# The phases of the states as one product in place of three, with every tile at a fixed place in two large tiles

## The chip, the cores and the metric

The kernel runs on one core of a Trainium2 chip. The metric is device time in microseconds of one execution. The kernel before took 527.39 us (median of three runs, 527.39 to 527.72).

The core has a matrix engine (PE; its weight loads are listed apart as PEld), a vector engine (DVE), a scalar engine (ACT), a general engine (POOL) and a queue engine (SP) that only issues DMAs. Each engine works through its own list of instructions in order. Where one needs another's result, it waits on a semaphore: the built program gives each waiting instruction a semaphore and the count that it must reach.

## The reference

One input `u` of 2048 rows by 640 channels goes through two branches, and a gate mixes them. Branch A is a convolution whose kernel K is a sum over 128 complex states per channel; branch B filters a two-dimensional Fourier transform.

```python
    def _A_ref(u, log_A_real, A_imag, C_real, C_imag, log_dt, D_skip):
        dt = jnp.exp(log_dt)
        A = -jnp.exp(log_A_real) + 1j * A_imag
        C = (C_real + 1j * C_imag) * dt[:, None]
        P = jnp.exp((A * dt[:, None])[:, :, None] * pos[None, None, :])
        K = 2.0 * jnp.einsum("dn,dnl->dl", C, P).real
        ...
        y = jnp.fft.irfft(Uf * Kf[None, :, :], L2)[:, :, :L]
        return y + u * D_skip[None, None, :]
    def _B_ref(x, w_r, w_i):
        X = jnp.fft.rfft2(x, axes=(-2, -1)) * (w_r + 1j * w_i)
        return jnp.fft.irfft2(X, s=(S, D), axes=(-2, -1))
    ...
    return g * a + (1 - g) * b
```

For each state the kernel needs the sine and cosine of an angle for all 2048 positions. It splits the position in an inner and an outer part, and forms each angle in turns. The whole turns have to be taken off before the sine: adding a large constant and taking it off again rounds the number of turns x to a whole one, and what is wanted is that whole number minus x.

## The kernel before, in words

There are four stages. **Phase A** (`phase_a`) transforms `u` over the positions and stores it to DRAM as `u_d`. **Phase P** (`phase_p`) prepares the parameters of the states and stores them, cut in three bfloat16 parts each, to the DRAM tensors `par_d0` (angles) and `par_d1` (decays). **Phase B** (`phase_b`) makes K from them, interleaved with **the channel branch** (`channels`, `filt`, `back1`, `back2`), which is the rest of branch B. **Phase D** (`phase_d`) transforms K (L370, then L383), multiplies it with the spectrum of `u` (L869, L870, L875), transforms back (L900, copied by ACT at L902), stores the half result to the DRAM tensor `s3_d` (L909), loads it in another layout as the tile `t3` (L948, in `load_c`) and finishes with the products at L973 and the gate.

Phase B runs over 40 tiles t, 16 channels each. Two products on the rows of `par1` and an exponential (`mags`, L709 and L710) give the decays `e`. Then `phases` makes the angles twice, for the outer part (`sc`, L725) and the inner part (L731). In `phases` (L713 to L720) three matrix products pile up in the same PSUM bank: with the first table come x and the rounding constant, with the second the constant's negative, with the third minus x. Each of the three is two products on 64 rows and 512 columns (partitions 0 to 63 and 64 to 127), so there are six at L719 for each call, and 80 calls. `prods` (L739 to L745) multiplies decays and angles on DVE and POOL, and `kgen` (L758) sums over the states. `load` brings `par1` (L696, two DMAs) and `par0` (L698, one DMA) for five tiles at a time, issued by POOL.

The tile `t3` spreads over the partitions in steps of four: each of its loads writes every fourth partition, 32 in all.

```python
                T.ld = eng.dma_start(t3s[c][y::4, :, a:a + w], src[:, :, a:a + w])
```

There are 16 such loads from SP and one from ACT. Of these, 15 move 640 KB and two (the halves of the last) 320 KB.

The order on every engine is written out by hand: `arrange` reads one list of numbers per engine (`ORDER`) and ties each engine's instructions in that order, and `CROSS` adds some ties between engines where two tiles share a place. Tiles come from pools of the framework, each a tensor of its own. The framework finds which accesses of a tensor overlap and sets the waits from that.

Of the kernel before, what the change touches and what calls it, by code (L numbers as in the profile page):

```python
# [9 lines left out]
F32 = mybir.dt.float32  # L10
BF = mybir.dt.bfloat16
# [3 lines left out]
PSUM = bass.MemoryType.PSUM  # L15
# [35 lines left out]
def _tables():  # L51
# [72 lines left out]
    one_row[:, :, 0] = 1.0  # L124
    rm = np.zeros((2, 64, 8, 96))
    rp = np.zeros((2, 32, 8, 128))
    for x in range(8):
        g, i = x // 4, 6 * (x % 4)
        rp[g, i:i + 3, x, 0:32] = rp[g, i:i + 3, x, 32:64] = j + 0.5
        rp[g, i:i + 3, x, 64:96] = rp[g, i:i + 3, x, 96:128] = 64 * j  # L130
        rp[g, i + 3:i + 6, x, 64:128] = 1.0
        rp[g, 24, x, 32:64] = rp[g, 24, x, 96:128] = -0.25
# [3 lines left out]
    rq = rp.copy()  # L136
    for x in range(8):
        rq[1 - x // 4, 24, x] = MAGIC
    flat = lambda v: np.concatenate([v[..., 0:64].reshape(64, 512), v[..., 64:128].reshape(64, 512)], 1)
    rn = np.zeros((64, 512))  # L140
    rn[24] = -MAGIC
    rp = np.tile(np.concatenate([flat(rq), rn, flat(-rp)], 1), (2, 1))
# [25 lines left out]
class Ctx:  # L168
    pass

# [28 lines left out]
def body(tc, A, out):  # L199
    nc = tc.nc  # L200
    T = Ctx()
    with ExitStack() as top:
        dram = top.enter_context(tc.tile_pool(name="dram", bufs=1, space=DRAM))
        T.u_d = dram.tile([4, 128, 17, 2, 160], F32, name="u_d")
# [22 lines left out]
        with ExitStack() as cctx:  # L227
            def left():
                with ExitStack() as ctx:
                    T.bc = ctx.enter_context(tc.tile_pool(name="b_c", reuse_waits="tile", bufs=1))  # L230
                    T.rm = T.bc.tile([128, 768], BF, name="rm")
                    T.rp = T.bc.tile([128, 2560], BF, name="rp")
                    yield from phase_p(tc, A, T)
                    yield from phase_b(tc, A, T, ctx)
# [13 lines left out]
            arrange(tc)  # L248
# [422 lines left out]
def phase_b(tc, A, T, ctx):  # L671
# [12 lines left out]
    par_v = [t.rearrange("y x i z n -> y (x i) z n") for t in T.par_d]  # L684
    steps = rp[:, 0:1024], rp[:, 1024:1536], rp[:, 1536:2560]
# [5 lines left out]
    def load(b0):  # L691
        for k in (1, 0):
            par = w2.tile([128, BT, N], BF, tag="par%d" % k, name="par%d" % k)
            if k:
                for j in range(2):
                    G.dma_start(par[64 * j:64 * j + 48], par_v[1][b0 // BT, 48 * j:48 * j + 48])  # L696
            else:
                G.dma_start(par[:, :, :], par_v[0][b0 // BT])  # L698
            for t in range(b0, b0 + BT):
                pars[k][t] = par[:, t - b0, :]  # L700
# [12 lines left out]
    def phases(t, c, n):  # L713
        p = ps.tile([128, 2, 512], F32, tag="ps", name="p_p")
        for i, w in enumerate(steps):
            y = 0 if i == 1 else c
            for j in range(2):
                x = slice(64 * j, 64 * j + 64)
                P.matmul(p[:, j, 0:n], pars[0][t][x], w[x, y:y + n], start=i == 0, stop=i == 2)  # L719
        return p  # L720

    def outer(t, r):
        p = phases(t, 512, 512)
# [4 lines left out]
    def inner(t, r):  # L728
        p = phases(t, 0, 512)
# [309 lines left out]
def arrange(tc):  # L1039

    nc, traced_by = tc.nc, {}
    for name, text in ORDER.items():
        traced = [i for i in nc.cur_bb.bb.instructions if i.engine == getattr(mybir.EngineType, name) and "Boundary" not in type(i).__name__]
        seq = []
        for part in text.split():
            a, _, n = part.partition("+")
            seq += traced[int(a):int(a) + int(n or 1)]
        assert len(seq) == len(traced) == len({i.name for i in seq})
        for a, b in zip(seq, seq[1:]):
            tc.add_manual_dep(b, a.name, NOSYNC, reason="order")  # L1050
        traced_by[name] = traced
    for pair in CROSS.split():
        (e, i), (f, j) = ((x[0], int(x[1:])) for x in pair.split(">"))
        tc.add_manual_dep(traced_by[LETTER[f]][j], traced_by[LETTER[e]][i].name, NOSYNC, reason="slot")


ORDER = {
    "PE": """
# [20 lines left out]
""",  # L1079
    "DVE": """  # L1080
# [74 lines left out]
```

## Time and profile before

| what | value |
|---|---|
| median of three runs | 527.39 us |
| profiled execution, first to last instruction | 526.1 us |
| granted PE clock, mean of the core | 0.992 |
| PE busy in the span | 492.4 us (94%) |
| DVE busy | 432.3 us (82%) |
| ACT busy | 308.1 us (59%) |
| POOL busy | 275.8 us (52%) |
| moved by DMA | 100.55 MB, mean 191 GB/s |

Times come from one profiled execution. Busy time is the union of an engine's instructions, idle time before an instruction is put down to what ended it, and the granted clock is the share of full speed that PE was given.

### The profile page before, as it was taken

How to read it: one execution, taken by the hardware profiler on the slowest of the kernel's cores; microseconds unless marked ns; L12 is line 12 of the kernel's file. 1: busy time of each engine (PE TensorE's matmuls, PEld its weight loads, DVE VectorE, ACT ScalarE, POOL GpSimd, SP SyncE). 2: the span in 40 equal slices, each digit the busy share in tenths (PEclk: the TensorE clock that was granted, in tenths of full speed). 3: DMA queues.
4: the chain of work that ended last, by engine and by line, in shares of the span. 5: the costliest groups of instructions: out<-in, count | busy, mean ns of one | idle time of the engine just before them, and what ended most of it. 6: DMA issues, size and time to landing. Idle time of an engine off the chain costs nothing. (4 is left out here: it accounts for less than half of the span.)

```text
span 526.1 us, 17188 instructions
## 1 busy us (share of the span) xinstructions
PE 492.4 (94%) x7448; PEld 365.2 (69%) x7448; DVE 432.3 (82%) x678; ACT 308.1 (59%) x484; POOL 275.8 (52%) x294
## 2 busy tenths in 40 slices
PE   8869999997889989999999899999999999999896
PEld 6859877765656656656656566757979879988641
DVE  0699757879999998999979869964797977979954
ACT  3566265577886787885976886877323333332210
POOL 4087626428637346476256345156452667538750
PEclk9989999999999999999989999999999999999999
DMA  8926753375251232541312421139689899889974
GB/s 337 403 103 212 284 184 116 106 241 186 78 198 52 75 109 67 190 141 52 98 61 62 165 60 29 56 121 411 215 293 349 276 328 329 296 265 355 310 257 173
DMA packets 47827, 100.55 MB, mean 191 GB/s; under 512 B 3620, under 2 KB 33080, under 8 KB 46088
## 3 DMA queue, kind: packets, MB, share of 16 engines
q1 hardware_dynamic: 25176, 67.41, 36.4%
q10 hardware_dynamic: 20080, 22.52, 13.0%
q0 software_dynamic: 2496, 9.54, 5.0%
q8 instruction: 58, 0.95, 0.7%
q14 instruction: 17, 0.14, 0.1%
HBM read 60.12 MB, written 39.65 MB: 190 GB/s over the span
## 5 line engine op out<-in xcount | busy, mean ns | idle before, releaser
L383 PE MATMUL p_s<-t,w 128*64 128x160 f32 x1056 | 89.0, 307 | 3.6 <-ACT ut L418 3.4
L383 PEld LDWEIGHTS p_s<-t,w 128*64 128x64 f32 x1056 | 75.6, 135 | 12.8 <-ACT ut L418 4.3
L744 POOL TENSOR_TENSOR y<-e,sc 128x512 f32<-128x512 f32 x40 | 53.4, 1335 | 34.5 <-ACT sc L725 34.4
L719 PE MATMUL p_p<-rp,par 64*128 64x512 bf16 x480 | 63.3, 382 | 5.7 <-ACT sc L725 2.6
L710 ACT ACTIVATE e<-p_e 128x1024 f32<-128x1024 f32 (+1 forms) x80 | 61.7, 823 | 9.4 <-issue 4.5
L745 POOL TENSOR_TENSOR y<-e,sc 128x512 f32<-128x512 f32 x40 | 53.5, 1338 | 21.7 <-ACT sc L725 21.6
L371 ACT COPY t<-p_s 128x512 f32<-128x512 f32 x40 | 25.1, 627 | 48.2 <-PE p_s L370 42.7
L731 ACT ACTIVATE p_p<-p_p 128x1024 f32<-128x1024 f32 x40 | 40.5, 1013 | 15.8 <-PE p_p L719 12.4
L741 DVE TENSOR_TENSOR x<-e,p_p 128x1024 f32<-128x1024 f32 x40 | 48.4, 1211 | 0.0
L902 ACT COPY s<-p_i 128x640 f32<-128x640 f32 x32 | 22.1, 692 | 39.6 <-PE p_i L900 33.4
L758 PEld LDWEIGHTS p_k<-x,y 128*32 128x32 f32 x2560 | 37.6, 110 | 10.5 <-issue 8.2
L758 PE MATMUL p_k<-x,y 128*32 128x64 f32 x2560 | 44.1, 220 | 0.1
L739 DVE SCALAR_TENSOR_TENSOR x<-e,p_p 128x512 f32<-128x512 f32 x40 | 27.2, 680 | 20.5 <-ACT p_p L731 20.5
L725 ACT ACTIVATE sc<-p_p 128x1024 f32<-128x1024 f32 x40 | 41.0, 1026 | 4.6 <-PE p_p L719 4.4
L719 PEld LDWEIGHTS <-par 64*128 64x128 bf16 x480 | 20.7, 95 | 32.2 <-issue 13.6
L900 PE MATMUL p_i<-t,w 128*64 128x160 f32 x528 | 42.2, 300 | 0.9 <-DVE t L875 0.7
L370 PE MATMUL p_s<-c,kt 128*64 128x128 f32 x640 | 42.6, 273 | 0.2 <-PE p_s L383 0.2
L875 POOL TENSOR_TENSOR t<-ma 64x320 f32<-64x320 f32 x32 | 28.4, 887 | 26.5 <-DVE ma L869 25.3
L370 PE MATMUL p_s<-c,u 128*64 128x128 f32 x640 | 39.4, 277 | 2.5 <-ACT t L418 2.3
L370 PEld LDWEIGHTS p_s<-c,kt 128*64 128x64 f32 x640 | 38.0, 136 | 4.3 <-issue 3.0
L900 PEld LDWEIGHTS p_i<-t,w 128*64 128x64 f32 x528 | 36.4, 136 | 6.5 <-issue 2.6
L370 PEld LDWEIGHTS p_s<-c,u 128*64 128x64 f32 x640 | 36.0, 138 | 6.6 <-issue 3.2
(165 smaller groups left out, 1017.2 us busy)
## 6 DMA issues: line engine op xcount, KB each, us to landing
u_d<-ut SPq DMA_DIRECT2D x32, 320.0 KB, 3.6
us<-u_d ACTq DMA_DIRECT2D x16, 640.0 KB, 5.5
s_d<-s ACTq DMA_DIRECT2D x15, 640.0 KB, 7.8
t<-s_d SPq DMA_DIRECT2D x14, 640.0 KB, 5.5
ww<-in_w_l SPq DMA_DIRECT2D x8, 642.0 KB, 4.3
ue<-u_d SPq DMA_DIRECT2D x8, 640.0 KB, 5.5
k_d<-kt SPq DMA_DIRECT2D x4, 1280.0 KB, 5.9
kt<-k_d SPq DMA_DIRECT2D x8, 640.0 KB, 6.0
```

Of the source, the lines that this page charges most:

```text
L370: nc.tensor.matmul(p[64 * ri:64 * ri + 64, j, :], src(i + j), e1[ri], start=True, stop=True)
L383: ins = nc.tensor.matmul(p[64 * j:64 * j + 64, i, 160 * ri:160 * ri + 160], w2[:, x, 64 * ri:64 * ri + 64], t1[:, x // 2 if x < 32 else K0 ...
L710: st.exp = S.activation(ef[:, :, c:c + n], p[:, :, 0:n], AF.Exp)
L719: P.matmul(p[:, j, 0:n], pars[0][t][x], w[x, y:y + n], start=i == 0, stop=i == 2)
L725: S.activation(sc.rearrange("p d v i -> p (d v i)"), p.rearrange("p j w -> p (j w)"), AF.Sin, scale=TWO_PI)
L731: T.trig = st.trig = S.activation(f, f, AF.Sin, scale=TWO_PI)
L741: V.tensor_tensor(out=x[:, 0].rearrange("p d (h j) -> p d h j", h=2), in0=e[:, :, 0:64].rearrange("p d (h j) -> p d h j", h=2), in1=cx.uns ...
L744: G.tensor_tensor(out=y[:, 1], in0=e[:, :, 64:96], in1=sc[:, 0], op=ALU.mult)
L745: G.tensor_tensor(out=y[:, 0], in0=e[:, :, 64:96], in1=sc[:, 1], op=ALU.mult)
L758: P.matmul(st.pb[32 * r:32 * r + 32, o, :], y[:, ri, 4 * qq + JR[r], :], x[:, ri, 4 * qq + JR[r], :], start=t % 2 + qq + 1 - ri == 0, stop ...
L875: return eng.tensor_tensor(out=t2[64 * im:64 * im + 64, o, :], in0=m[l, :hn, 0, :], in1=m[l, :hn, 1, :], op=ALU.add if im else ALU.subtract)
L900: T.mm = P.matmul(p[x:x + 64, i // 2, 160 * (i % 2):160 * (i % 2) + 160], T.w3[:, k0 + h + i, x:x + 64], t2[:, h + i, :], start=True, stop ...
```

## The change

Two things change. First, the products of `phases`: each angle row now stands in the table as x in rows 0 to 23, the quarter turn in row 24, the constant in row 25, its negative in row 26 and minus x in rows 32 to 63, so that one product per half does what three did. The eight tables become four, the columns of a product 256 instead of 512, and the parameters come in two groups g side by side in the free dimension. The tile `rp` shrinks from 2560 to 512 columns, `par0` doubles, and its load becomes four DMAs.

```diff
-    one_row[:, :, 0] = 1.0
+    one_row[:, :, 0:3] = 1.0
...
+    rp[32:64] = -rp[0:32]
+    rp[25], rp[26] = MAGIC, -MAGIC
...
-                G.dma_start(par[:, :, :], par_v[0][b0 // BT])
+                    for x in (0, 32):
+                        G.dma_start(par[64 * j + x:64 * j + x + 32], T.par_d[0][b0 // BT, 2 * j:2 * j + 2].rearrange("g i z n -> i g z n"))
...
-        for i, w in enumerate(steps):
-            y = 0 if i == 1 else c
+        for g in range(2):
             for j in range(2):
                 x = slice(64 * j, 64 * j + 64)
-                P.matmul(p[:, j, 0:n], pars[0][t][x], w[x, y:y + n], start=i == 0, stop=i == 2)
+                P.matmul(p[:, j, n * g:n * g + n], pars[0][t][x, g], rp[x, c:c + n], start=True, stop=True)
```

Second, how the program is written down. `body` no longer calls the framework: a class `Program` records every operation, `lay` gives each pool a stretch of addresses, and `write` then issues the operations in one list of numbers for all engines, putting each tile at a place in two tiles that fill the whole memories, `sbuf` and `psum`. `arrange` and the ties of `CROSS` are gone.

```diff
+        for s, n in self.SIZE.items():
+            pool = self.area.enter_context(self.tc.tile_pool(name=s, bufs=1, **({"space": PSUM} if s == "psum" else {})))
+            area[s] = pool.tile([128, n // 4], F32, name=s)
...
+                x = area[s][:, h.slot[1] // 4:h.slot[1] // 4 + size]
...
+        for n in order:
+            op = self.ops[n]
...
-            arrange(tc)
+        tc.write(sequence(ORDER))
```

Line by line, the instructions of DVE, ACT and SP stand in the same order as before. On PE only the products of `phases` differ, on POOL only the loads of the parameters. What differs besides is what instructions wait for. Three places follow; the words in brackets are the semaphores that an instruction waits for, one for each engine and some (DMAHW, DMASW) for DMAs.

On POOL, near the start of phase B, these are the first loads of the parameters before (par_521 and par_1015 are `par1`, par_524 and par_1018 are `par0`).

```order
L430 TENSOR_TENSOR z<-c_66,gw 128x640 [waits PE_49,Pool_49]
L696 DMA par_1015<-par_d_62 48x640 [waits DMASW1_49]
L696 DMA par_1015<-par_d_62 48x640 [waits DMASW2_49]
L698 DMA par_524<-par_d_61 128x640 [waits DMASW6_49,DMASW5_49]
L698 DMA par_1018<-par_d_61 128x640
```

The same place of the changed kernel, where every tile on the chip is called sbuf or psum:

```order
L865 DMA sbuf<-par_d_62 48x640 [waits DMASW1_49]
L865 DMA sbuf<-par_d_62 48x640 [waits DMASW2_49]
L868 DMA sbuf<-par_d_61 32x2x640 [waits DMASW6_49,DMASW5_49]
L868 DMA sbuf<-par_d_61 32x2x640 x3
L868 DMA sbuf<-par_d_61 32x2x640 [waits DMASW7_49]
L868 DMA sbuf<-par_d_61 32x2x640 [waits DMASW0_49]
```

Each load at L698 is now four at L868, and the later ones of the eight wait for the loads just ahead.

On SP in phase D, these are the first loads of `t3` before (L948; t_6040 is `t3`, s_d is `s3_d`), between those of K (L816) and of another tile (L936).

```order
L936 DMA t3e<-s3e_d 128x2560 [waits DMAHW4_49,DMAHW1_49,PE_49]
L948 DMA t_6040<-s_d 32x5120 [waits DMAHW3_49,DMAHW0_49,DVE_49]
L816 DMA kt<-k_d 128x1280 [waits DMAHW7_49,PE_49,Pool_49]
L948 DMA t_6040<-s_d 32x5120 [waits DMAHW4_49]
L948 DMA t_6040<-s_d 32x5120 [waits DMAHW3_49,DMAHW2_49]
```

The same place of the changed kernel, in which L1117 is L948, L985 is L816 and L1105 is L936:

```order
L1105 DMA sbuf<-s3e_d 128x2560 [waits DMAHW4_49,DMAHW1_49,PE_49]
L1117 DMA sbuf<-s_d 32x5120 [waits DMAHW2_49,DMAHW1_49,DMAHW3_49,DMAHW0_49,DMAHW5_49,DVE_49,DMAHW6_49,PE_49,DMAHW7_49,Activation_49,Pool_49]
L985 DMA sbuf<-k_d 128x1280 [waits DMAHW3_49,PE_49]
L1117 DMA sbuf<-s_d 32x5120 [waits DMAHW5_49,DMAHW4_49,DMAHW6_49,DVE_49,DMAHW7_49,Activation_49,Pool_49]
L1117 DMA sbuf<-s_d 32x5120 [waits DVE_49,DMAHW1_49,PE_49,DMAHW2_49,Activation_49,Pool_49]
```

The loads stand where they stood. The first now waits for all eight semaphores of SP's and ACT's DMAs but one, and for all four engines; the counts in the built program are those of the instruction that stands just ahead of the load in the list, on each engine.

On PE, at the same place, these are the products of the back transform before (L900; p_i_5877 and p_i_5891 are two PSUM banks, t_5659 the spectrum).

```order
L900 MATMUL p_i_5877<-t_5659,w_5003 64x160 [waits DMAHW5_49]
L900 MATMUL p_i_5877<-t_5659,w_5003 64x160
L900 MATMUL p_i_5891<-t_5659,w_5003 64x160 [waits Activation_49,Pool_49]
L900 MATMUL p_i_5891<-t_5659,w_5003 64x160 x7
L383 MATMUL p_s_5907<-t_5012,w_69 64x160 [waits DVE_49]
```

The same of the changed kernel (L1069 is L900, L553 is L383):

```order
L1069 MATMUL psum<-sbuf 64x160 [waits DMAHW5_49]
L1069 MATMUL psum<-sbuf 64x160
L1069 MATMUL psum<-sbuf 64x160 [waits DVE_49]
L1069 MATMUL psum<-sbuf 64x160 x4
L1069 MATMUL psum<-sbuf 64x160 [waits DMAHW3_49]
L1069 MATMUL psum<-sbuf 64x160 x2
L553 MATMUL psum<-sbuf 64x160 [waits Activation_49]
```

The eight products of the second bank are cut in two: the sixth now waits for DMAHW3_49, the semaphore that the first load of `t3` raises when it has landed. ACT, DVE and POOL have such a wait at the same place in the list. So it is at each of the 17 loads, on every engine that has work behind it.

More of the change, by code (lines that the diff above doesn't have):

```diff
@@ L1 @@
 import math
-from contextlib import ExitStack, nullcontext
+import sys
+from contextlib import ExitStack
+from functools import partial
 import numpy as np
@@ L135, in _tables @@
         rm[:, 6 * x + 3:6 * x + 6, x, 64:96] = 1.0
[L136 to L142, printed above, removed]
+    rp = np.tile(np.concatenate([rp[..., 0:64].reshape(64, 256), rp[..., 64:128].reshape(64, 256)], 1), (2, 1))
     f = lambda x: np.ascontiguousarray(x, dtype=np.float32)
@@ L169, with __init__, then, __getitem__ @@
     pass
+class View:
+    def __init__(self, home, steps=()):
+        self.home, self.steps = home, steps
+    def then(self, *step):
+        return View(self.home, (*self.steps, step))
+    def __getitem__(self, x):
+        return self.then("__getitem__", x)
+    def rearrange(self, text, **sizes):
+        return self.then("rearrange", text, sizes)
+    def unsqueeze(self, x):
+        return self.then("unsqueeze", x)
+    def broadcast_to(self, x):
+        return self.then("broadcast_to", x)
+    def bitcast(self, x):
+        return self.then("bitcast", x)
+    def real(self, base):
+        x = base
+        for name, a, *k in self.steps:
+            x = x[a] if name == "__getitem__" else getattr(x, name)(a, **(k[0] if k else {}))
+        return x
@@ new lines, with __init__ @@
+class Home(View):
+    def __init__(self, tag, shape, dtype, name):
+        super().__init__(self)
+        self.tag, self.shape, self.dtype, self.name = tag, tuple(shape), dtype, name
+        self.left, self.slot = 0, None
+        size = int(np.prod(self.shape[1:])) * mybir.dt.size(dtype)
+        tag.size = max(tag.size, -(-size // tag.step) * tag.step)
+class Tag:
+    def __init__(self, space, bufs):
+        self.space, self.bufs, self.size = space, bufs, 0
+        self.step = 2048 if space == "psum" else 32
@@ new lines, with __init__, __enter__, __exit__ @@
+class Pool:
+    def __init__(self, program, bufs, space, side):
+        self.program, self.bufs, self.space, self.side, self.tags = program, bufs, space, side, {}
+    def __enter__(self):
+        self.program.events.append((self, 1))
+        return self
+    def __exit__(self, *_):
+        self.program.events.append((self, 0))
+    def tile(self, shape, dtype, name, tag=None):
+        t = self.tags.setdefault(tag or name, Tag(self.space, self.bufs))
+        return Home(t, shape, dtype, name)
@@ new lines, with __init__, __getattr__, record @@
+class Engine:
+    def __init__(self, program, name):
+        self.program, self.name = program, name
+    def __getattr__(self, op):
+        def record(*a, **k):
+            self.program.ops.append((self.name, op, a, k, sys._getframe(1).f_lineno))
+            return len(self.program.ops)
+        return record
+def views(op):
+    return [x for x in (*op[2], *op[3].values()) if isinstance(x, View)]
+class Program:
+    SIZE = {"sbuf": 212832, "psum": 16384}
+    def __init__(self, tc):
+        self.tc, self.nc, self.ops, self.events = tc, self, [], []
+        for x in ("sync", "scalar", "vector", "gpsimd", "tensor"):
+            setattr(self, x, Engine(self, x))
+    def tile_pool(self, name, bufs=1, space=None, side="left", reuse_waits=None):
+        return Pool(self, bufs, "psum" if space == PSUM else "sbuf", side)
+    def lay(self):
+        at = {(s, d): 0 if d == "left" else self.SIZE[s] for s in self.SIZE for d in ("left", "right")}
+        held = {}
+        for pool, opened in self.events:
+            k = pool.space, pool.side
+            if not opened:
+                at[k] = held[pool]
+                continue
+            held[pool] = at[k]
+            for t in pool.tags.values():
+                n = t.size * t.bufs
+                lo = at[k] if pool.side == "left" else at[k] - n
+                t.slots = [(lo + i * t.size, lo + i * t.size + t.size) for i in range(t.bufs)]
+                at[k] = lo + n if pool.side == "left" else lo
+            assert at[pool.space, "left"] <= at[pool.space, "right"], (pool.space, at)
+    def write(self, order):
+        self.lay()
+        nc = self.tc.nc
+        area = {}
+        for s, n in self.SIZE.items():
+            pool = self.area.enter_context(self.tc.tile_pool(name=s, bufs=1, **({"space": PSUM} if s == "psum" else {})))
+            area[s] = pool.tile([128, n // 4], F32, name=s)
+        for op in self.ops:
+            for h in {v.home for v in views(op)}:
+                h.left += 1
+        used, last, lines = {}, {}, {}
+        def place(h, n):
+            s = h.tag.space
+            if h.slot is None:
+                def since(slot):
+                    over = [x for x in used if x[0] == s and x[1] < slot[1] and slot[0] < x[2]]
+                    return None if any(used[x] for x in over) else max([last[x] for x in over], default=-1)
+                free = [(t, slot) for slot in h.tag.slots if (t := since(slot)) is not None]
+                assert free, ("no slot", h.name, n)
+                h.slot = (s, *min(free)[1])
+                used[h.slot] = 1
+                size = int(np.prod(h.shape[1:])) * mybir.dt.size(h.dtype) // 4
+                x = area[s][:, h.slot[1] // 4:h.slot[1] // 4 + size]
+                x = x if h.dtype == F32 else x.bitcast(h.dtype)
+                if len(h.shape) > 2:
+                    d = "abcde"[:len(h.shape) - 1]
+                    x = x.rearrange("p (%s) -> p %s" % (" ".join(d), " ".join(d)), **dict(zip(d[1:], h.shape[2:])))
+                h.base = x
+            return h.base
+        for n in order:
+            op = self.ops[n]
+            e, name, a, k, line = op
+            r = lambda x: x.real(place(x.home, n)) if isinstance(x, View) else x
+            call = lines.setdefault(line, compile("call()", __file__, "eval").replace(co_name="line%d" % line, co_firstlineno=line))
+            eval(call, {"call": partial(getattr(getattr(nc, e), name), *map(r, a), **{i: r(x) for i, x in k.items()})})
+            for h in {v.home for v in views(op)}:
+                h.left -= 1
+                if not h.left:
+                    used[h.slot], last[h.slot] = 0, n_out(nc)
+        prev = {}
+        for i in nc.cur_bb.bb.instructions:
+            if "Boundary" not in type(i).__name__:
+                e = str(i.engine)
+                if e in prev:
+                    self.tc.add_manual_dep(i, prev[e].name, NOSYNC, reason="order")
+                prev[e] = i
@@ L172, in halved, with n_out, sequence @@
+def n_out(nc):
+    return len(nc.cur_bb.bb.instructions)
+def sequence(text):
+    out = []
+    for part in text.split():
+        a, _, n = part.partition("+")
+        out += range(int(a), int(a) + int(n or 1))
+    return out
 def halved(nc, out, w, x):
@@ L203, in body @@
         dram = top.enter_context(tc.tile_pool(name="dram", bufs=1, space=DRAM))
+        tc = nc = Program(tc)
+        tc.area = top
         T.u_d = dram.tile([4, 128, 17, 2, 160], F32, name="u_d")
@@ L683, in phase_b @@
     rp, rm = T.rp, T.rm
-    par_v = [t.rearrange("y x i z n -> y (x i) z n") for t in T.par_d]
-    steps = rp[:, 0:1024], rp[:, 1024:1536], rp[:, 1536:2560]
+    par_v = T.par_d[1].rearrange("y x i z n -> y (x i) z n")
     es, pars, xy, rs = {}, ({}, {}), {}, {}
@@ L692, in load @@
         for k in (1, 0):
[L693 to L698, printed above, removed]
+            par = w2.tile([128, 2 - k, BT, N], BF, tag="par%d" % k, name="par%d" % k)
+            for j in range(2):
+                if k:
+                    G.dma_start(par[64 * j:64 * j + 48, 0], par_v[b0 // BT, 48 * j:48 * j + 48])
+                else:
+                    for x in (0, 32):
+                        G.dma_start(par[64 * j + x:64 * j + x + 32], T.par_d[0][b0 // BT, 2 * j:2 * j + 2].rearrange("g i z n -> i g z n"))
             for t in range(b0, b0 + BT):
-                pars[k][t] = par[:, t - b0, :]
+                pars[k][t] = par[:, 0, t - b0, :] if k else par[:, :, t - b0, :]
     def mags(t):
@@ L728, in inner @@
     def inner(t, r):
-        p = phases(t, 0, 512)
+        p = phases(t, 0, 256)
         f = p.rearrange("p j w -> p (j w)")
@@ L1036, in phase_d @@
         run(last_c(3, a))
[L1039 to L1054, printed above, removed]
@@ L1132 @@
[L1132 removed]
+ORDER = """
[111 rows of a table added]
 """
```

43 lines of the change are left out of this document (9 added, 34 removed), and 162 rows, old and new, of the table ORDER.

## The prediction

> **What bounds the kernel now.** I read the page's sums and slices first, for the engine that is busiest and for the clock that it was granted.
>
> ```profile
> span 526.1 us, 17188 instructions
> PE 492.4 (94%) x7448; PEld 365.2 (69%) x7448; DVE 432.3 (82%) x678; ACT 308.1 (59%) x484; POOL 275.8 (52%) x294
> ...
> PE   8869999997889989999999899999999999999896
> ...
> PEclk9989999999999999999989999999999999999999
> ```
>
> PE is busy nearly all the time at full clock. An average says little about a stage, so next come the busy times by stage: phase B with the channel branch, and phase D from its first load of t3 to the tail. The columns are PE, PEld, DVE, ACT, POOL, the granted clock, the DMA share and GB/s.
>
> ```profile
> 120.00:370.00 250.00, 235.59 (x3636) 157.46 (x3637) 223.41 (x351) 197.56 (x310) 131.04 (x139) 0.99 0.35 117
> ...
> 397.30:512.00 114.70, 111.72 (x1373) 92.23 (x1370) 94.46 (x147) 35.17 (x56) 69.45 (x77) 1.00 0.91 308
> ```
>
> In phase B, PE has 14 us of slack and DVE 27. In phase D, PE idles 3.0 of 114.7 us: that stage is bound by PE, and it is full only because the DMA engines (0.91 busy) work beside it. The waits show how well the loads of t3 are hidden there.
>
> ```profile
> SPq L948 <- DMA s_d<-s: 62.0, 13, 10.5
> PE p_c L973 <- DMA t<-s_d: 1.1, 1, 1.1
> ```
>
> SP waits 62 us in all for the stores that a load of t3 reads, and it costs nothing, as nobody else waits on SP. PE loses 1.1 us in all to t3.
>
> **The products of phases (gain).** The rows are those of the products and their weight loads, and, with shapes kept apart, of the 256-column product at L709, the form that the new products have.
>
> ```profile
> L719 PE MATMUL p_p<-rp,par 64*128 64x512 bf16 x480 | 63.3, 382 | 5.7 <-ACT sc L725 2.6 <-DVE x L741 2.5 <-ACT e L710 0.5
> ...
> L719 PEld LDWEIGHTS <-par 64*128 64x128 bf16 x480 | 20.7, 95 | 32.2 <-issue 13.6 <-DVE x L741 1.7
> ...
> L709 PE MATMUL p_e<-rm,par 48*128 48x256 bf16 x80 | 11.3, 278 | 4.0 <-ACT e L710 2.1 <-DVE x L741 1.5
> ```
>
> The 480 products keep PE busy for 63.3 us, which is 0.79 us for each of 80 calls, or 0.26 for a pair of 512 columns (the halves run side by side). A call becomes two pairs of 256 columns. A pair costs 0.28 at most (11.3 us over 40 pairs at L709) and 0.13 at least (half of 0.26). I take 0.19, two weight loads of 95 ns one after the other, which lies between. So a call goes from 0.79 to 0.38, and PE is freed of 80 x 0.41 = 33 us (18 to 42).
>
> Not all of that is time. DVE's work stays, and in phase B it idles 250 - 223.4 = 26.6 us, so no more than about 26 us can go before DVE is late next. Its list and ACT's keep their order, which was laid out for the slower products. I take **10 us off**, with 0 and 26 as ends.
>
> The parameters' loads become 32 DMAs on POOL where there were 8.
>
> ```profile
> L698 POOL DMA_DIRECT2D par<-par_d x8 | 4.8, 597 | 1.7 <-PE p_e L709 1.0 <-issue 0.4 <-PE p_p L719 0.3
> ```
>
> At 0.6 us each that is 24 x 0.6 = 14 us more on POOL, 1.8 at each of eight places. POOL has 119 us free in phase B, and the y products queued behind a load wait for ACT anyhow; I count nothing. Without that cover each of the seven places after the first would cost up to 1.8 us, 13 in all, which would eat the gain. The smaller rp only moves less data at the start, and I count nothing for it.
>
> **The fixed places (loss).** All tiles on the chip are now views of one tensor, so what the framework takes for an overlap decides the waits. A load of t3 writes every fourth partition. In the built program it waits for the last instruction ahead of it in the list on every engine and for every DMA still under way, and the next instruction of every engine waits until it has landed. I take this for a stride over partitions that is treated as covering all columns between its first and last partition. Whatever the reason, the rows of the order show the waits, and the counts in the program are the latest ones. Each of the **17 loads is a barrier** in a stage that had none. I found no other new wait whose releaser ends over 0.5 us after the waiting instruction's start in the trace of before, but for two early parameter loads on POOL (1.7 us, t is needed later).
>
> The price of a barrier has four terms. **Drain**: the engines do not cross a cut together. The timeline around the first cut (start, duration, engine) has these rows:
>
> ```profile
> 395.77 2.11 PE L900 MATMUL p_i<-t,w 128*64 128x160 f32 x28
> ...
> 397.12 1.05 DVE L875 TENSOR_TENSOR t<-mb 64x320 f32<-64x320 f32 x1
> ...
> 396.56 0.33 ACTq L856 DMA_DIRECT2D us<-u_d  x1
> ```
>
> The cut lies in the second half of PE's eight last products, at about 397.5; DVE's last operation ahead of it ends at 398.2. That is 0.7 us in which PE has nothing. Where POOL still follows DVE it is more.
>
> ```profile
> L979 POOL TENSOR_TENSOR ot<-ot,oe 128x480 f32<-128x480 f32 (+1 forms) x17 | 18.5, 1105 | 15.0 <-issue 12.3 <-DVE ot L978 2.6
> ```
>
> With one such operation behind it would be 1.8; I take 1.1.
>
> **DMAs under way**: the load of us was issued at 396.56. Its like, and the stores to s3_d, take from issue to landing (least, median, most of L856, then L909, then L948, the loads of t3):
>
> ```profile
> DMA to landing us min/median/max: 3.8/5.5/14.4
> ```
>
> ```profile
> DMA to landing us min/median/max: 2.7/6.3/12.1
> ```
>
> ```profile
> DMA to landing us min/median/max: 4.4/4.8/8.9
> ```
>
> With 5.5 us it lands at 402.1, 3.9 after the drain. Nine of the 17 cuts have such a DMA issued less than 3 us ahead of them, the first at 396.56 and the last this store:
>
> ```profile
> 504.35 0.37 ACTq L909 DMA_DIRECT2D s_d<-s  x1
> ```
>
> At some 3.3 us each, 9 x 3.3 / 17 = 1.7 us a barrier; the ends are 0 and 3.9.
>
> **The load itself**: 4.8 us by its median, and 0.2 for SP's waits and the engines' resuming, a guess; 5.0. The ends are 4.4 and the longest that the chain of waits holds:
>
> ```profile
> 422.58 6.97 DMA t<-s_d
> ```
>
> The two half loads take some 1.5 us less each: half stores to s3_d at 320 KB landed in 2.7 us where 640 KB took a median of 7.8.
>
> ```profile
> s_d<-s ACTq DMA_DIRECT2D x15, 640.0 KB, 7.8
> ...
> s_d<-s ACTq DMA_DIRECT2D x2, 320.0 KB, 2.7
> ```
>
> **The clock**: PE now idles 1.1 + 1.7 + 5.0 = 7.8 us at a time. Before, its idle time of 2.5 us ahead of 30.23 was followed by this (stages and timeline):
>
> ```profile
> 28.00:29.50 1.50, 0.00 (x0) 0.00 (x0) 1.50 (x5) 0.38 (x1) 1.10 (x1) 1.00 0.31 113
> 29.50:33.00 3.50, 2.77 (x20) 2.50 (x22) 3.47 (x3) 2.05 (x6) 3.41 (x3) 0.51 0.28 108
> 33.00:35.00 2.00, 2.00 (x41) 2.00 (x40) 2.00 (x3) 1.41 (x2) 1.92 (x2) 1.00 0.55 181
> ```
>
> ```profile
> 30.23 2.13 PE L383 MATMUL p_s<-t,w 128*64 128x160 f32 x11 [2.54 <-ACT ut L418]
> ```
>
> The clock fell to half for 3.5 us and then came back. I count one such stretch a barrier: 3.5 us at half clock loses 1.7. The ends are 0 and 3.5 (two stretches).
>
> [...]
>
> **Sum**: 1.1 + 1.7 + 5.0 + 1.7 = 9.5 us, times 17 is 161.5, less 3 for the half loads 158.5. The span goes to 526.1 - 10 + 158.5 = 674.6 us. The median of the runs before lies 1.3 us above that span (527.4 against 526.1), so the time is **676 us**.
>
> Between barriers the work itself stays as it was: 111.7 us of PE, all inputs landed. The eight idle products at L1032 stay too.
>
> **The rivals.** *The waits cost nothing* (this ends faster). If the counts were long reached when SP comes to a load, and the load landed ahead of its next neighbours, only the gain would be left: 527.4 - 10 = 517, between 501 and 527. It decides where SP gets to a load more than 5 us ahead of the engines. For it speaks that PE lost only 1.1 us to t3 before. Against it: a load that waits for the instruction just ahead cannot be early, and SP waited 62 us for these loads even with far fewer waits. I give it 5%. *Nothing either way*: with the gain eaten by POOL's loads on top, 527; 1%.
>
> [...]
>
> *Cheap barriers.* DMA engines that were 0.91 busy are nearly idle when a load goes out alone: load 4.4, nothing under way, drain 0.5, clock 0.8 is 5.7, times 17 is 97 less 3, so 527 - 10 + 94 = 611. For it: the quiet load from ACT near the end took 4.4. Against it: DMAs stand just ahead of nine cuts. 6% for 528 to 625.
>
> **How the numbers follow.** The likeliest, 676, has 80% within 625 to 735. A price of 6.6 a barrier with 10 gained gives 626, one of 12.8 with nothing gained gives 742; I cut there, since not all four terms end high at once. All ends low or high together would be 591 to 800. Faster by over 0.2% (what a measurement of this kernel can tell from no change): 5%; within: 1%; slower: 94%.
>
> **What would show it.** In the profile after: 17 gaps of PE of 6 us or more behind 397, each ended by a DMA of t3; SP waiting for PE, DVE, POOL and ACT at the loads; the clock at about half behind each gap; DMA's share in phase D well under 0.91; phase B shorter by about 10 us, with L719's group near 30 us. If the gaps are missing, the reading of the order was wrong. If they are there and 4 us long, the price of the load was; if phase B is not shorter, the gain was.

## The result, and the profile after

The changed kernel takes 675.56 us (median of 4 executions, 670.65 to 676.04) against 527.56 us before: a ratio of 1.2767, with a 95% interval of 1.2719 to 1.2815. The forecast was 676. Ratios here and below leave out executions more than 1.5% above the fastest of their kernel. The profiled execution took 675.82 us, with a span of 673.8.

The page of the changed kernel, its sums and two of its rows of 40 slices (PE and the clock that it was granted):

```profile
span 673.8 us, 17031 instructions
PE 515.7 (77%) x7288; PEld 394.7 (59%) x7288; DVE 431.2 (64%) x678; ACT 307.8 (46%) x484; POOL 290.0 (43%) x318
...
PE   8889998879889997988979954769376556556464
...
PEclk9899999999999998898799987888677668788777
```

DVE and ACT do as much as before (431.2 and 307.8 us). PE has 160 matmuls fewer and is busy 23 us longer, and the last two fifths of both rows have fallen. The busy times of phase D, from PE's last product ahead of the first load of t3 to the end, say the same; the columns are length, PE, PEld, DVE, ACT, POOL, clock, DMA share, GB/s. Before:

```profile
397.50:526.10 128.60, 120.74 (x1406) 94.97 (x1402) 100.19 (x165) 34.97 (x56) 69.25 (x77) 0.99 0.86 293
```

After:

```profile
394.60:673.80 279.20, 163.88 (x1407) 125.57 (x1406) 100.15 (x165) 35.48 (x56) 68.59 (x77) 0.77 0.41 135
```

The same work takes 150.6 us more. DMA's share halves, PE idles 115 us, and its 1,400 products themselves take 43.1 us more, at a mean clock of 0.77. The waits of PE in the changed kernel (total us, times, longest) name the releaser:

```profile
PE psum L553 <- DMA sbuf<-s_d: 29.0, 4, 8.6
PE psum L1069 <- DMA sbuf<-s_d: 25.2, 4, 8.1
PE psum L1142 <- DMA sbuf<-s_d: 15.7, 3, 5.7
PE psum L540 <- DMA sbuf<-s_d: 13.5, 2, 7.4
PE psum L553 <- ACT sbuf L541: 11.5, 1, 11.5
PE psum L888 <- DVE sbuf L910: 7.3, 11, 1.9
PE psum L1201 <- ACT sbuf L1071: 6.9, 1, 6.9
...
PE psum L344 <- DMA sbuf<-s_d: 4.9, 1, 4.9
```

"DMA sbuf<-s_d" is the load of t3 (line 1117 now). L553 belongs to the transform of K (L383 before) and L1069 is the transform back (L900 before). Neither reads anything of t3: they wait for a load that they do not need. (In the two ACT rows ACT resumed first behind the load, and PE waited for ACT.) The timeline of the changed kernel around the first of them:

```profile
392.50 2.10 PE L1069 MATMUL psum<-sbuf 128*64 128x160 f32 x26
...
393.45 1.70 DVE L1044 TENSOR_TENSOR sbuf<-sbuf 64x320 f32<-64x320 f32 x2
393.56 0.33 ACTq L1025 DMA_DIRECT2D sbuf<-u_d  x1
398.31 0.49 SPq L1117 DMA_DIRECT2D sbuf<-s_d  x1
...
402.63 1.06 PE L1069 MATMUL psum<-sbuf 128*64 128x160 f32 x5 [8.02 <-DMA sbuf<-s_d]
402.66 0.69 ACT L1071 COPY sbuf<-psum 128x640 f32<-128x640 f32 x1 [9.30 <-DMA sbuf<-s_d]
```

This is read as the four terms of the prediction. PE stops at 394.6 and DVE at 395.15: 0.55 us of **drain**. The load of us, issued at 393.56, is still **under way**, so SP issues the load of t3 only at 398.31, 3.16 us later. The **load** lands, and PE goes on at 402.63, 4.32 after the issue. Then PE works at half **clock**: 0.50 was granted from 397.7 to 407.9 (that is in the 43.1 us). SP's waits in the changed kernel show that such transfers, loads of us and stores to s3_d, often come last there:

```profile
SPq L1117 <- DMA s_d<-sbuf: 19.8, 7, 7.9
...
SPq L1117 <- DMA sbuf<-u_d: 11.9, 4, 6.9
```

Read in the same way as at this first load, all 17 loads give:

| per load | forecast, us | measured, mean of 17 (sum) |
|---|---|---|
| drain | 1.1 | 0.86 (14.5) |
| DMAs under way | 1.7 | 1.55 (26.3) |
| the load, to PE's resuming | 4.8 (5.0, half loads less) | 4.08 (69.4) |
| PE's gap | 7.6 | 6.48 (110.2) |
| half clock (PE's longer work) | 1.7 | 2.5 (43.1) |
| other idle time of PE | 0 | -0.2 (-2.7) |
| sum of phase D | 9.3 (158.5) | 8.9 (150.6) |
| gain ahead of it | 10 | 2.9 in this execution |

The gain is the shift of the first gap: PE stops at 394.6 where the cut stood at 397.5.

### The profile page after: what moved, and what is told of

It reads as the page before. It is cut to its first block, busy times and chain, and to the rows that moved or that the text cites. A ratio compares the mean times of both kernels' runs of the same rounds, so it can differ in the third digit from the quotient of the medians.

```text
span 673.8 us, 17031 instructions
## 1 busy us (share of the span) xinstructions
PE 515.7 (77%) x7288; PEld 394.7 (59%) x7288; DVE 431.2 (64%) x678; ACT 307.8 (46%) x484; POOL 290.0 (43%) x318
## 5 line engine op out<-in xcount | busy, mean ns | idle before, releaser
L553 PE MATMUL psum<-sbuf 128*64 128x160 f32 x1056 | 108.1, 337 | 44.1 <-DMA sbuf<-s_d 29.0
L553 PEld LDWEIGHTS psum<-sbuf 128*64 128x64 f32 x1056 | 89.8, 152 | 55.9 <-DMA sbuf<-s_d 21.4
L1044 POOL TENSOR_TENSOR sbuf<-sbuf 64x320 f32<-64x320 f32 (+1 forms) x68 | 61.6, 905 | 117.8 <-DVE sbuf L1038 67.6
L540 PE MATMUL psum<-sbuf 128*64 128x128 f32 x1280 | 94.9, 292 | 15.9 <-DMA sbuf<-s_d 13.5
L540 PEld LDWEIGHTS psum<-sbuf 128*64 128x64 f32 x1280 | 85.4, 147 | 23.7 <-DMA sbuf<-s_d 14.0
L1038 DVE TENSOR_TENSOR sbuf<-psum,sbuf 128x640 f32<-128x640 f32 (+1 forms) x36 | 28.2, 784 | 88.0 <-PE psum L553 81.6
L1069 PE MATMUL psum<-sbuf 128*64 128x160 f32 x528 | 56.8, 337 | 25.4 <-DMA sbuf<-s_d 25.2
L913 POOL TENSOR_TENSOR sbuf<-sbuf 128x512 f32<-128x512 f32 x40 | 53.4, 1335 | 32.9 <-ACT sbuf L894 30.8
L880 ACT ACTIVATE sbuf<-psum 128x1024 f32<-128x1024 f32 (+1 forms) x80 | 61.7, 819 | 9.6 <-PE psum L879 9.2
L1069 PEld LDWEIGHTS psum<-sbuf 128*64 128x64 f32 x528 | 46.7, 155 | 32.0 <-DMA sbuf<-s_d 26.4
L740 PE MATMUL psum<-sbuf 128*128 128x160 f32 (+2 forms) x280 | 62.6, 345 | 3.3 <-ACT sbuf L729 1.0
L914 POOL TENSOR_TENSOR sbuf<-sbuf 128x512 f32<-128x512 f32 x40 | 54.7, 1369 | 15.8 <-ACT sbuf L894 13.7
L910 DVE TENSOR_TENSOR sbuf<-sbuf,psum 128x1024 f32<-128x1024 f32 x40 | 48.4, 1209 | 0.0
L1044 DVE TENSOR_TENSOR sbuf<-sbuf 64x320 f32<-64x320 f32 (+1 forms) x68 | 42.9, 639 | 7.3 <-DMA sbuf<-s_d 6.6
L927 PE MATMUL psum<-sbuf 128*32 128x64 f32 x2560 | 47.1, 229 | 0.3 <-ACT sbuf L933 0.2
L900 ACT ACTIVATE psum<-psum 128x1024 f32<-128x1024 f32 x40 | 40.8, 1020 | 8.3 <-PE psum L888 8.2
```

Source lines behind the costliest of these rows:

```text
L540: nc.tensor.matmul(p[64 * ri:64 * ri + 64, j, :], src(i + j), e1[ri], start=True, stop=True)
L553: ins = nc.tensor.matmul(p[64 * j:64 * j + 64, i, 160 * ri:160 * ri + 160], w2[:, x, 64 * ri:64 * ri + 64], t1[:, x // 2 if x < 32 else K0 ...
L740: P.matmul(out, src(c), tab[0], start=first, stop=not first)
L880: st.exp = S.activation(ef[:, :, c:c + n], p[:, :, 0:n], AF.Exp)
L910: V.tensor_tensor(out=x[:, 0].rearrange("p d (h j) -> p d h j", h=2), in0=e[:, :, 0:64].rearrange("p d (h j) -> p d h j", h=2), in1=cx.uns ...
L913: G.tensor_tensor(out=y[:, 1], in0=e[:, :, 64:96], in1=sc[:, 0], op=ALU.mult)
```

## The experiments

Lateness below is the start of DVE's n-th instruction less the start of the same one in the profile of before; DVE has the same 678 instructions in the same order in each of these kernels.

**t3_blocks: the waits away, by another layout.**

```diff
-        e1[0], e1[1], e3.reshape(4, 32, 64).swapaxes(0, 1).reshape(128, 64), e3e.reshape(128, 128), np.eye(128), one,
+        e1[0], e1[1], e3.reshape(128, 64), e3e.reshape(128, 128), np.eye(128), one,
...
-                T.ld = eng.dma_start(t3s[c][y::4, :, a:a + w], src[:, :, a:a + w])
+                T.ld = eng.dma_start(t3s[c][32 * y:32 * y + 32, :, a:a + w], src[:, :, a:a + w])
```

> The changed kernel, but each load of t3 writes 32 successive partitions instead of every fourth, with the rows of the table e3 put in the same order; nothing else differs. In the built program the loads no longer wait for every engine, and no engine waits for them all. Theory (the 17 waits are the whole loss, and 3.0 us were gained ahead of the first of them): 527.5 - 3.0 = 524.5 us, between 522 and 527; no PE gap over 3 us behind 397, DMA share of phase D again near 0.9. Rival 1 (the fixed places cost something besides these waits, through slots that come free later): 530 to 560. Rival 2 (a load over 32 neighbouring partitions is itself slower): also over 530, with the landings of these loads well above 4.0 us.

Measured: 542.29 us (539.24 to 544.14), ratio 1.0271 (1.0243 to 1.0299). The stretch that the waits had broken up is nearly full again (columns as above):

```profile
397.00:512.00 115.00, 106.31 (x1333) 88.20 (x1329) 91.99 (x144) 33.24 (x53) 67.83 (x76) 1.00 0.99 283
```

So 133 of the 148 us go with the stride, but the kernel is still 18 us over the theory.

**before_blocks: the same layout in the kernel before.** The same two lines, here line 948 and the line of the tables.

> The kernel before, with only that change of t3's loads and of e3's rows. Theory: the layout of the load is worth nothing by itself, 527.5 us within 1. Rival 2 (the layout costs): slower by what the run with fixed places loses, over 530.

Measured: 543.15 us, ratio 1.0307 (1.0273 to 1.0341). Rival 2 holds: the layout costs about as much without fixed places. The landings of its loads of t3 (issue to landing, which a trace gives for five of the 17 loads; they were 4.4/4.8/8.9 with the stride):

```profile
DMA to landing us min/median/max: 5.5/7.2/11.8
```

In t3_blocks they were 5.9/7.2/11.8. Much of the loss comes at the tail, where little other work stands beside the loads: in t3_blocks DVE is 1.6 us late at 494 and 13.3 at its last instruction, in before_blocks 7.5 and 14.8. So t3_blocks has to be held not against the kernel before, but against before_blocks. There it is 0.9 us faster by the medians, with its lighter products; what the places cost by themselves, the next run asks.

**three_products: the fixed places with the old products.** As t3_blocks, with

```diff
-        for g in range(2):
+        m = []
+        for i, y in enumerate((c, 1024, 1536 + c)):
...
-                P.matmul(p[:, j, n * g:n * g + n], pars[0][t][x, g], rp[x, c:c + n], start=True, stop=True)
+                m.append(((p[:, j, 0:n], pars[0][t][x], rp[x, y:y + n]), dict(start=i == 0, stop=i == 2)))
+        for q in (m[0:2], m[2:3], m[3:5], m[5:6]):
+            P.matmul(*q[0][0], **q[0][1], more=q[1:])
```

The six products of a call are collected in `m` and issued in four places of the list, so that the order of everything else stays.

> As t3_blocks, but with the three products of 512 columns of before (and its tables) in place of the one of 256; the parameter loads stay four. So the fixed places stand alone. Theory: the places alone cost nothing without the waits, 527.5 us within 1.5, and the clock as before (one half-rate stretch of 3.4 us near 265). The difference to t3_blocks is what the products bring: 3 us by the trace of the changed kernel. Rival 1: over 530.

Measured: 545.56 us (541.92 to 548.82), ratio 1.0333 (1.0297 to 1.0370). By its number the theory failed, as in t3_blocks, by the layout's 15 us. Against before_blocks (1.0273 to 1.0341) the places show no cost that is clear of the noise: 2.4 us by the medians, and the intervals overlap. The difference to t3_blocks, 3.3 us, is what was expected of the products.

**one_product and one_product_again: the products alone, in the kernel before.** Its pools and order stay, and with them the stride without the waits:

```diff
-        for i, w in enumerate(steps):
-            y = 0 if i == 1 else c
+        for g in range(2):
...
-                P.matmul(p[:, j, 0:n], pars[0][t][x], w[x, y:y + n], start=i == 0, stop=i == 2)
+                m = P.matmul(p[:, j, n * g:n * g + n], pars[0][t][x, g], rp[x, c:c + n], start=True, stop=True)
```

> The kernel before with the products' part of the change alone: one product in place of three, its tables and the 24 more parameter loads, in the pools and the order of before, t3 loaded to every fourth partition as there. No load of t3 waits for every engine. Theory (the 17 waits are the loss, the products a small gain whose greater part the clock takes back): three_products against t3_blocks gave 545.6 - 542.3 = 3.3 us, so 527.7 - 3.3 = 524.4, between 522 and 526. Rival (the gain hung on the fixed places): 527 to 529.

> one_product once more, beside the next two, since its six executions spread from 518 to 531 us and the profiled one was the longest. Theory (the clock decides how much of the products' lead is kept, execution by execution): again between 518 and 531, median near 521, and in the profiled one DVE's lead over the kernel before shrinks only where PE runs at half clock. Rival (the spread came from disturbed runs): all within 1.5 us of 520.

Measured: 520.84 us, ratio 0.9843 (0.9796 to 0.9891), and 524.1 us, ratio 0.9895 (0.9864 to 0.9927). It is the version that beats both kernels, by less than 2%. The gain does not hang on the places, and at 3.4 to 6.6 us of the medians it is at least the 3.3 expected; the first median lies below its range, the second above the 521 expected of it. The twelve executions spread from 518.3 to 530.9 us, and the mean granted clock parts them: the six at 0.974 or more took 518.3 to 521.8, the six below it 522.9 to 530.9. Three of these, at 529.5 to 530.9, are slower than the median of the kernel before. In the profile of one_product_again (519.0 us of span) DVE is 5.5 us early at 267 and 6.9 at 395. In that of one_product (529.0) it is 5.6 early at 267 and 3.7 late at 395.

**twice, one_product_twice, one_product_some: PE kept busier.** In twice and one_product_twice each product is issued twice, in one_product_some only

```diff
+                if t in (25, 26, 27, 32, 33, 34):
+                    m = P.matmul(p[:, j, n * g:n * g + n], pars[0][t][x, g], rp[x, c:c + n], start=True, stop=True)
...
```

> As t3_blocks, but each of the 320 products of phases is issued twice in a row (the second overwrites the first with the same numbers), so that PE is about as busy as with three products. It asks why a lead of 8 us at 265 shrank to 1 at 350 in the changed kernel, where PE ran at half clock for 10.2 and 13.7 us. Theory (the freed PE idles, so its clock is halved, and that gives the gain back): the stretches at half clock go or shrink to one of 3.4 us; if the lead of 8 is kept, 519 to 521 us, and if the doubled products cost what they did before, 527. Rival (the half clock has nothing to do with PE's idleness): both stretches stay, and the time is that of t3_blocks or up to 4 us above it.

> As one_product, with each product issued twice as in the run called twice, which was 5.0 us faster than t3_blocks. Theory (PE that idles less keeps its clock): 524.4 - 5.0 = 519.4, between 517 and 522, and at most one stretch of half clock between 200 and 390. Rival (that difference was chance): as one_product or slower.

> As one_product, but the products of six of the 40 calls (t = 25 to 27 and 32 to 34, around the places where the changed kernel fell to half clock for 10.2 and 13.7 us) are issued twice. Theory (PE's idle time at these two places is what halves its clock): no stretch of half clock over 3.4 us between 255 and 345, a lead of 5 us or more at 354, and the slow executions of one_product are missing: 517 to 521. Rival (PE's busy share there does not decide it): the stretches and the spread of one_product stay, 518 to 531.

Measured: 537.34 us for twice (0.9% under t3_blocks, ratio 1.0188, 1.0164 to 1.0212), the way its theory had it, though its numbers, 519 to 527, were missed by the layout's 15 us. Its mean clocks were 0.977 to 0.981 where t3_blocks had 0.952 to 0.962, and DVE was still 7.5 us early at 395. But one_product_twice took 525.48 (0.9937, 0.9905 to 0.9968) and one_product_some 522.78 (0.9922, 0.9892 to 0.9951). Both are over their theories (517 to 522 and 517 to 521), neither is better than one_product, and both had a mean clock from 0.96 to 0.99. What doubling spares in clock it can cost in work. Whether PE's idle time is what lets the clock fall in phase B stays open.

**thin_loads: the load's part.** The changed kernel, stride and waits kept, with

```diff
-                T.ld = eng.dma_start(t3s[c][y::4, :, a:a + w], src[:, :, a:a + w])
+                T.ld = eng.dma_start(t3s[c][y::4, :, a:a + 3], src[:, :, a:a + 3])
...
-                P.matmul(p[64 * x:64 * x + 64, 0:n], T.e3, t3[:, x, a + i:a + i + n], start=True, stop=True)
+                P.matmul(p[64 * x:64 * x + 64, 0:n], T.e3, t3[:, x, 0:n], start=True, stop=True)
```

> The changed kernel, but each load of t3 fetches only three of its columns a (3/16 of the bytes, 120 KB), and all products of e3 read those three; so it leaves out most of that data, the work and the 17 waits stay. It weighs the load's own part of a wait. Theory (the landing, 4.0 us of a gap of 6.5, is what costs): the nearest rows, loads of 60 to 320 KB, landed in 2.6 to 2.9, so 1.3 us less each, 17 x 1.3 = 22 us, and somewhat less at half clock: 645 to 656 us. Rival (drain and DMAs under way are what costs): over 665.

Measured: 634.64 us, ratio 1.2006 (1.1924 to 1.2087), below the 645 to 656 of the theory. Its loads landed in

```profile
DMA to landing us min/median/max: 2.3/2.3/2.4
```

The 17 gaps sum to 83.0 us where they were 110.2, and drain (14.5) and DMAs under way (26.7) are what they were: all 27 us come off the load's own term, as the theory said, at 1.6 us a load where I had 1.3. The span is 41 us shorter, not 27, since in this execution the lead ahead of the first load was 12.4 us and not 3.0, and the clock lost less (a mean of 0.904 against 0.881). The load is the largest term, but three fifths of it (2.5 of 4.1 us) stay with a fifth of the bytes.

**four_waits: four of the 17.** As t3_blocks, with the stride kept for one quarter:

```diff
+                rows = slice(y, 128, 4) if c == 0 else slice(32 * y, 32 * y + 32)
+                T.ld = eng.dma_start(t3s[c][rows, :, a:a + w], src[:, :, a:a + w])
...
+                P.matmul(p[64 * x:64 * x + 64, 0:n], T.e3 if c == 0 else T.e3b, t3[:, x, a + i:a + i + n], start=True, stop=True)
```

> As t3_blocks, but the four loads of t3 of the first quarter (c = 0) write every fourth partition again; a second copy of e3 serves the others. So four waits of every engine come back, the rest stay away. Theory (each wait has its own price, whatever the others do): in the changed kernel DVE lost 33.5 + 3.0 = 36.5 us over the first four, so 542.3 + 36.5 = 579, between 570 and 588. Rival (the price is high only because 17 stand close together and the clock does not get warm between them): 542.3 + 4 x 6 = 566 or less.

Measured: four executions from 560.35 to 575.06 us, median 571.13, too wide for an interval; 29 us over t3_blocks by medians, 21 by the fastest of each. PE's waits in the profiled one:

```profile
PE psum L554 <- DMA sbuf<-s_d: 14.8, 2, 8.6
PE psum L1070 <- DMA sbuf<-s_d: 8.8, 1, 8.8
...
PE psum L344 <- DMA sbuf<-s_d: 4.9, 1, 4.9
```

They are four gaps of 28.5 us together, against 27.7 for the first four of the changed kernel (8.02, 8.57, 4.90, 6.17). Over them DVE loses 35.9 us, and 36.0 in the changed kernel. So a gap has its price whether 4 stand there or 17. The full 36.5 us I had was too much as a difference to t3_blocks, as that kernel itself loses 3.7 us over this stretch; how much of the rest is clock, this spread does not settle.

**t3_chunks: fixed places, another way without a stride.**

```diff
-        e1[0], e1[1], e3.reshape(4, 32, 64).swapaxes(0, 1).reshape(128, 64), e3e.reshape(128, 128), np.eye(128), one,
+        e1[0], e1[1], e3.reshape(4, 4, 8, 64).swapaxes(0, 1).reshape(128, 64), e3e.reshape(128, 128), np.eye(128), one,
...
-                T.ld = eng.dma_start(t3s[c][y::4, :, a:a + w], src[:, :, a:a + w])
+                m = [((t3s[c][32 * q + 8 * y:32 * q + 8 * y + 8, :, a:a + w], src[8 * q:8 * q + 8, :, a:a + w]), {}) for q in range(4)]
+                T.ld = eng.dma_start(*m[0][0], more=m[1:])
```

> The changed kernel with fixed places, but each load of t3 is four loads of eight successive partitions, 32 partitions apart, and e3's rows stand accordingly; so the partitions are spread as widely as with every fourth, without a stride, and no load waits for every engine. It asks why t3_blocks was 15 us slower than its waits explain. Theory (a load to 32 neighbouring partitions is slow because they lie together): as one_product, 518 to 526. Rival (what made t3_blocks slow is something else, or four small loads take as long): 535 to 545.

Measured: 656.62 us, ratio 1.231 (1.2263 to 1.2356), slower than either forecast. No load waits for every engine, but PE waits for the data:

```profile
PE psum L1145 <- DMA sbuf<-s_d: 96.8, 3, 39.8
```

L1145 is the product that does read t3. While it waited, the stretch looked like this (columns as above):

```profile
576.00:605.00 29.00, 0.12 (x2) 0.15 (x4) 0.00 (x0) 0.00 (x0) 0.00 (x0) 0.50 0.52 62
```

The DMA engines move 62 GB/s, with no compute engine at work. A share of 0.52 of 16 engines is some eight transfers at a time, and eight is what one of the four loads has, one for each of its partitions. By this the four go one after the other, an estimate from that share, and a spread over four loads does not help here.

## Why the prediction was right, and where it was not

**The mechanism.** The waits of the 17 loads are the loss. Away from them (one_product) the same products in the old places make the kernel 1.0 to 1.6% faster; with them it is 28% slower. That they come from the stride over partitions, which I only took for so, is shown by t3_blocks: the same tensor and the same slots, rows in a block, and 133 us go. None of the rivals came: the waits were neither free nor cheap (8.9 us each, where the cheap barrier had 5.7). The clock came back behind every one of them, after 3.4 to 13.7 us at half; that lost 40.8 us in all.

**The price of a wait.** Forecast 9.3 with the half loads, measured 8.9. Drain and DMAs under way were met within 0.25 us. The load was too dear, 4.8 where 4.1 was measured: I took the median landing of before, 4.8, though a load that goes out alone could land sooner, which I had given to the cheap rival. The 4.4 that I took there, of ACT's load before, was not of a quiet time: the DMA share from 504.90 to 509.30 was 0.87. The half loads saved 0.8 us each where I had 1.5. A load now takes (five of the 17 again)

```profile
DMA to landing us min/median/max: 3.6/4.0/4.1
```

The clock was too cheap, 1.7 for 2.5: one stretch of 3.5 us at half clock was the count, and a gap brought more. By the clock's records in the trace the 17 stretches last 3.4 to 13.7 us and hold 81.6 us of PE's work, 4.8 a load. That accounts for 40.8 of the 43.1 us. Over all terms, the load (13 us), drain, DMAs under way and other idle time were 22 us too dear, the clock (14) and the gain (7) 21 too cheap. That the sum is right within 1 us is owed to their signs, and is luck.

**The gain: 10 us forecast, 2.9 in the profile.** This is the step that was furthest off. Its first half held, PE and POOL in the changed kernel:

```profile
L888 PE MATMUL psum<-sbuf 64*128 64x256 bf16 x320 | 30.2, 280 | 13.1 <-DVE sbuf L910 7.3 <-ACT sbuf L894 3.6 <-ACT sbuf L880 2.1
...
L868 POOL DMA_DIRECT2D sbuf<-par_d x32 | 17.4, 550 | 0.7 <-PE psum L888 0.6
```

The products fell from 63.3 to 30.2 us, 33.1 where 33 was said, and the 24 more loads of the parameters cost POOL 12.6 us and PE nothing that the page shows. DVE, too, gained what was expected, for a while. One and the same instruction before:

```profile
266.58 0.37 DVE L630 SCALAR_TENSOR_TENSOR qq<-o,c,p_eo 128x160 f32<-128x160 f32 x1
...
343.16 0.36 DVE L630 SCALAR_TENSOR_TENSOR qq<-o,c,p_eo 128x160 f32<-128x160 f32 x1
```

and after:

```profile
258.94 0.38 DVE L800 SCALAR_TENSOR_TENSOR sbuf<-sbuf,psum 128x160 f32<-128x160 f32 x1
...
342.29 0.36 DVE L800 SCALAR_TENSOR_TENSOR sbuf<-sbuf,psum 128x160 f32<-128x160 f32 x1
```

The lead is 7.6 us at 267 and 0.9 at 343. Between them lie two stretches of the changed kernel at half clock, shown with the one between (columns as above):

```profile
264.60:274.80 10.20, 10.20 (x104) 7.27 (x102) 6.91 (x11) 3.18 (x7) 7.14 (x7) 0.50 0.01 2
274.80:315.80 41.00, 35.77 (x610) 25.65 (x606) 34.79 (x56) 34.41 (x55) 21.48 (x22) 1.00 0.30 97
315.80:329.40 13.60, 13.60 (x177) 9.30 (x174) 9.66 (x17) 6.20 (x9) 3.05 (x3) 0.50 0.11 25
```

PE has no idle time in the first and third and runs at half clock, so the stage waits for it. The lead goes there: it is 8.4 us at 263 and 4.9 at 280, then 5.9 at 307 and 0.9 at 338. I had a term for the clock behind the waits and none in phase B. That it goes with the clock and not with the products is also seen in other profiles with the same products. From 250 to 370 the clock was 0.90 in the changed kernel and 0.97 in thin_loads, whose lead grew to 12.4 us; it was 0.89 in one_product, which lost its lead and 3.7 us more, and 0.96 in one_product_again, which kept it. No run sets the clock by itself, so this is seen in the runs and not tried. A lead of 6.9 and 12.4 us at 395 where the clock stayed up says that 10 was a fair size, and what was missing is that the clock can take back some 9 us of it, more or less from execution to execution.

**What would have shown it.** Seventeen gaps came, but ten, not all, are 6 us or longer: the shortest, 3.39, is that of a half load with nothing under way. DMA's share (0.41), the clock and L719's successor (30.2 us) read as announced; phase B was not 10 us shorter.

## What to carry to other kernels

When tiles become views of one tensor, look in the built order for instructions that wait for every engine: one transfer with a stride over partitions was enough to stop all of them, at 8.9 us a time. Before a stride is taken out to be rid of such a wait, ask what it was there for; here it spread the load over the partitions, and without it the same bytes landed 1.5 times as late. A gain on the busiest engine was only worth its full size here where the engine's clock stayed up (at 395 a lead of 12.4 us with 0.97 from 250 to 370, 3.0 with 0.90), so read the clock beside the lead, in more than one execution.

## What the hardware showed that was not expected

**Which partitions a load writes decides its speed here.** 640 KB to every fourth partition landed in 4.0 us alone and in a median of 4.8 beside other work; to 32 neighbouring partitions, 7.2 beside other work and never under 5.5; to eight at a time, the DMA engines moved 62 GB/s. The traces' records of the single transfers of t3, 20,480 bytes to one partition each, say the same. Their median is 0.77 us in the kernel before, 1.51 in t3_blocks and 2.47 in t3_chunks. Up to 18 of them run at a time in the first two and at most 9 in t3_chunks, so there fewer run side by side and each is slower as well. Why the partitions differ, no run here shows.

**PE can stay at half clock though it never idles.** In the two stretches above it was busy, as far as the profile's modelled ends of matmuls tell, for 10.20 of 10.20 us and 13.60 of 13.60 and was not given its full clock. The longest gaps ahead of the first stretch were these two:

```profile
261.82 0.39 PE L888 MATMUL psum<-sbuf 64*128 64x256 bf16 x4 [0.92 <-ACT sbuf L894]
...
263.74 0.54 PE L740 MATMUL psum<-sbuf 128*128 128x161 f32 x2 [1.05 <-ACT sbuf L729]
```

In the kernel before, the clock's records have one such stretch at this place, of 3.4 us from 265.1. Behind the 17 waits of phase D the clock came back after 3.4 to 13.7 us, and here after 10.2 and 13.7. What decides how long a stretch lasts, no run here shows.
